# Dummy matmuls in TensorE's early gaps, and later planned times for TensorE's users of transfers, in an attention kernel that feeds an MLP

## The chip, the cores and the metric

The kernel runs on one core of a Trainium2 chip. The core has a matrix engine (TensorE, "PE" in the profile), a vector engine (VectorE, "DVE"), a scalar engine (ScalarE, "ACT"), GpSimd ("POOL") and SyncE ("SP", here only a queue that starts transfers), and 16 DMA engines. Each engine works through its own instruction list in order; semaphores tell one engine that another is done. The metric is the device time of one execution in microseconds (us); lower is better.

## The reference

Eight batches of eight heads, 576 tokens, 64 values per head. Sixteen "beacon" keys and values stand in front of each batch's own. The attention output, 4608 rows of 512 values, goes through a two-layer MLP with a squared relu:

```
k_all = concat([beacon_k, k]);  v_all = concat([beacon_v, v])          # 592 keys
scores = q @ k_all.T / 8;  later keys masked, the beacon keys never
a = exp(scores - max);  a /= a.sum() + 1e-9
x = (a @ v_all), heads side by side                                     # [4608, 512]
h = x @ w_in;  g = relu(h) ** 2;  out = g @ w_out                       # d_ff = 2048
```

Inputs and the output are float32; the kernel computes its matmuls in bfloat16.

## The kernel before

**Tiling.** Keys lie in five tiles (four of 128, one of 80). A pair is two heads; there are 4 pairs per batch and 32 in all. For a pair, TensorE computes the scores with keys on the partitions (L589, op `qk`, into one of two PSUM strips, two matmuls side by side on the two halves of the array), ScalarE takes the exponential into a `pt` tile (L604), VectorE clears the masked part (L614, L618), TensorE multiplies with v (L639, op `av`; v carries a column of ones, which gives the row sums), and VectorE divides (L657, L659, op `norm`). The MLP runs in nine chunks of 512 tokens. A chunk's first layer is 16 steps `s1` (L770, four matmuls of 512 columns each; in chunk 0 two parts), then relu (L786 on ScalarE or L788 on VectorE) and square (L795); its second layer is 4 token tiles of 4 steps `s2` (L805, again four matmuls of 512 columns), an eviction into `osb` and a store (L831, L833, "OUT" below). An `s1` or `s2` step of four 512-column matmuls is called a **quad** below, as is an `s1` step that is cut in two because its tokens wrap around the ring of `xT`.

**Batch 0** is worked in two parts, so that it can start on a part of the tokens: part one is tokens 0 to 239, part two the rest. Its q and k for part one come by the SP and ACT queues (L487), are cast and transposed on TensorE (L451); part two comes by the POOL queue (L419) and is transposed at L454. Batch 1 comes by L419 too. From batch 2 on, q and k come through staging tiles `stg` (eight of them) by the SP queue (L344), are cast on POOL (L299) into `qk_area`, and are transposed by two DMA transposes per batch (L376, ops `trq` and `trk`, each a transfer that the SP queue issues). v comes by L344 too and is cast on POOL into `vb` (L299). From batch 3 on the attention output is transposed into `xT` by five DMA transposes per batch on the SP queue (L690, op `xt`); they wait for the batch's last `norm`. The loads of batch 2 wait until the last quarter of `w_out` has landed.

**What sets the order.** Nothing runs at the listed order of the loops. At build time every piece of work is an `Op` with engines, a duration, a priority and needs, and `Order.run` (lines 67 to 179) plays them through a list of events: whenever an engine is free it takes the released op with the lowest priority number. The sequence that comes out is then written down, one fixed list per engine and queue. Durations in it are the author's figures. A transfer takes `dma` us on one shared DMA time line after a start latency, and counts as seen 1.6 us after that; its users are released at that moment. What the chip then does with the lists is not known to the planner: an engine whose next instruction is not ready waits, and everything behind it waits too.

The names that the change touches: `add_load` (L328, casts of q, k, v), `add_trans` (L372), `add_beacon` (L386), `add_part_loads` (L412), `add_strided` (L429), `add_first_loads` (L477), `add_xt` (L683), and `Order.run`. `g[1]` is the relu buffer of odd chunks, not used before chunk 1; `strips[1]` is the second score strip.

The softmax here doesn't subtract the row's maximum and nothing guards it: scores larger than these inputs give would overflow.

## Time and profile before

| | |
|---|---|
| median of 5 runs | 345.83 us (345.3 to 347.62) |
| profiled execution, its own time | 347.62 us |
| its span, first to last instruction | 345.9 us |
| TensorE busy | 327.6 us, 95% |
| ScalarE / VectorE / GpSimd busy | 194.7 / 169.8 / 90.5 us |
| moved by DMA | 51.88 MB |
| last matmul starts / span ends | 341.5 / 345.9 us |

The profiled execution was the slowest of the five by its own time; its span is 1.7 us shorter than that time. Times in the text are microseconds from the start of the span. A row of the timeline gives start, duration, engine, line, operation, tiles, shape and count, and in brackets how long the engine was idle before it and what ended that. "SPq" and "POOLq" are the queues' own work of issuing transfers. A matmul's end is modelled, so rows overlap by some tenths.

Read off the trace for later use, in us: when the last of the 16 parts of a transfer landed, and when its first user on TensorE started.

| batch | trk issued | trk landed | first scores start | last v cast ends | first `av` starts |
|---|---|---|---|---|---|
| 2 | 67.27 | 73.08 | 73.56 | 82.54 | 81.25 |
| 3 | 93.98 | 100.51 | 101.58 | 108.67 | 108.67 |
| 4 | 122.22 | 127.28 | 129.44 | 135.06 | 136.73 |
| 5 | 155.63 | 160.51 | 163.15 | 174.87 | 173.95 |
| 6 | 188.56 | 196.65 | 197.05 | 208.81 | 207.89 |
| 7 | 223.02 | 227.96 | 229.15 | 242.30 | 241.68 |

The last quarter of `w_out` landed at 50.12. An `av` step needs the last v tile only in its last matmul.

### The profile page before, as it was taken

Reading aid. Unit: us, or ns where it says so; the run is one execution under the profiler, and the core shown is the slowest. Engines: PE = TensorE matmul, PEld = TensorE weight load, DVE = VectorE, ACT = ScalarE, POOL = GpSimd, SP = SyncE. Lnnn points to the kernel's source line nnn. Section 1 sums busy time; section 2 is a strip of 40 time slices with the busy share of each in tenths; the row PEclk is TensorE's granted clock in tenths of the full one; section 3 lists DMA queues with packets and bytes.
Section 4 is the critical chain, followed back from the end, with each engine's and each line's share of the span. In section 5 each row is a group of like instructions: output and inputs, shape, how many; then the busy total and the mean of one; then the engine's idle time right before and its main releaser. Section 6 shows DMA issues by size and latency. Waiting matters only on the chain.

```text
span 345.9 us, 7128 instructions
## 1 busy us (share of the span) xinstructions
PE 327.6 (95%) x2829; PEld 174.1 (50%) x2868; DVE 169.8 (49%) x372; ACT 194.7 (56%) x297; POOL 90.5 (26%) x141
## 2 busy tenths in 40 slices
PE   2799999999999999999999999999999999999995
PEld 1467675544554454444456855544554444444442
DVE  5787984147644974385355546456533302401400
ACT  3795774276646765576566655577536416515611
POOL 9844803305514514150153014312000000000000
PEclk9999999999999999999999999999999999999998
DMA  7999979999999999898799979994015011011002
GB/s 158 210 206 216 206 122 191 211 241 208 189 217 217 213 184 176 198 229 174 152 243 203 178 144 200 217 225 107 2 61 131 0 61 63 0 61 63 0 20 101
DMA packets 145291, 51.88 MB, mean 150 GB/s; under 512 B 132458, under 2 KB 140010, under 8 KB 145258
## 3 DMA queue, kind: packets, MB, share of 16 engines
q1 hardware_dynamic: 135741, 42.45, 59.6%
q0 software_dynamic: 8512, 8.49, 14.7%
q10 hardware_dynamic: 1005, 0.49, 0.5%
q8 instruction: 22, 0.36, 0.4%
q14 instruction: 11, 0.09, 0.1%
HBM read 37.22 MB, written 9.44 MB: 135 GB/s over the span
## 4 chain that ended last, share of the span: by engine, by line
PE 74%; DMA 11%; SPq 4%; ACT 3%; DVE 3%; POOL 2%; issue 1%; POOLq 0%; DVEq 0%; ACTq 0%
PE ps L805 32%; PE ps L770 28%; PE ps L639 8%; DMA stg<-in_v_dram 7%; PE strip L589 6%; SPq L690 3%; ACT pt L604 2%; DMA stg<-in_q_dram 2%; DMA osb<-in_k_dram 1%; DMA out_dram<-osb 1%; POOL vb L299 1%; SPq L344 1%; PE ps L707 1%; DVE g L795 1%; ACT g L786 1%
## 5 line engine op out<-in xcount | busy, mean ns | idle before, releaser
L770 PE MATMUL ps<-xT,w_in 128*128 128x512 bf16 (+3 forms) x690 | 133.2, 340 | 0.8 <-DVE qT L299 0.2
L805 PE MATMUL ps<-w_out,g 128*128 128x512 bf16 x551 | 131.2, 379 | 1.9 <-issue 0.8
L604 ACT ACTIVATE pt<-strip 128x832 bf16<-128x832 f32 (+4 forms) x128 | 103.6, 867 | 39.7 <-PE strip L589 39.7
L786 ACT ACTIVATE g<-ps 128x512 bf16<-128x512 f32 (+2 forms) x128 | 72.0, 562 | 46.6 <-PE ps L770 46.1
L770 PEld LDWEIGHTS <-w_in 128*128 128x128 bf16 x704 | 65.2, 98 | 56.0 <-issue 4.9
L795 DVE TENSOR_TENSOR g<-g 128x1024 bf16<-128x1024 bf16 (+2 forms) x80 | 52.4, 658 | 76.5 <-ACT g L786 75.2
L805 PEld LDWEIGHTS <-g 128*128 128x128 bf16 x576 | 52.4, 98 | 60.8 <-issue 4.0
L299 POOL CAST qk_area<-stg 128x512 bf16<-128x512 f32 (+2 forms) x60 | 39.8, 667 | 56.6 <-DMA stg<-in_k_dram 35.2
L299 POOL CAST vb<-stg 128x512 bf16<-128x512 f32 (+1 forms) x38 | 25.3, 675 | 83.8 <-DMA stg<-in_v_dram 66.3
L297 ACT COPY osb<-ps 128x512 f32<-128x512 f32 x26 | 15.2, 586 | 50.8 <-PE ps L805 44.5
L639 PEld LDWEIGHTS <-pt 128*128 128x128 bf16 (+1 forms) x960 | 36.4, 98 | 14.6 <-issue 3.5
L639 PE MATMUL ps<-vb,pt 128*128 128x65 bf16 (+1 forms) x960 | 40.6, 194 | 1.8 <-POOL vb L299 1.6
L589 PE MATMUL strip<-qT,kT 64*128 64x80 bf16 (+7 forms) x400 | 36.0, 283 | 1.9 <-ACT pt L604 0.6
L659 DVE TENSOR_TENSOR xn<-ps,rcp 128x320 bf16<-128x320 f32 (+2 forms) x64 | 31.5, 492 | 2.5 <-DVE rcp L657 0.2
L614 DVE TENSOR_TENSOR pt<-pt,tri 128x1024 bf16<-128x1024 bf16 (+1 forms) x36 | 24.6, 683 | 13.8 <-ACT pt L604 13.8
L657 DVE RECIPROCAL rcp<-ps 128x5 f32<-128x5 f32 (+2 forms) x64 | 12.2, 191 | 32.1 <-PE ps L639 31.9
L788 DVE TENSOR_SCALAR g<-ps 128x512 bf16<-128x512 f32 (+2 forms) x32 | 19.0, 598 | 10.0 <-PE ps L770 9.3
L589 PEld LDWEIGHTS <-kT 64*128 64x128 bf16 x400 | 12.7, 95 | 21.6 <-issue 16.9
L299 DVE COPY osb<-ps 128x512 f32<-128x512 f32 x10 | 6.9, 692 | 15.4 <-PE ps L805 13.6
L618 DVE TENSOR_TENSOR pt<-pt,tri 80x160 bf16<-80x160 bf16 x32 | 11.5, 359 | 0.0
L344 POOL DMA_DIRECT2D stg<-in_v_dram x10 | 8.6, 863 | 8.5 <-DMA w_in<-in_moe_w_in_dram 6.6
L451 PE MATMUL ps<-ident,qk_area 120*128 120x120 bf16 x16 | 2.3, 300 | 7.6 <-DVE qk_area L299 7.5
(39 smaller groups left out, 69.7 us busy)
## 6 DMA issues: line engine op xcount, KB each, us to landing
out_dram<-osb SPq DMA_DIRECT2D x17, 512.0 KB, 3.4
stg<-in_q_dram SPq DMA_DIRECT2D x24, 256.0 KB, 5.1
stg<-in_k_dram SPq DMA_DIRECT2D x18, 256.0 KB, 5.1
stg<-in_v_dram SPq DMA_DIRECT2D x18, 256.0 KB, 4.5
w_in<-in_moe_w_in_dram POOLq DMA_DIRECT2D x4, 512.0 KB, 11.3
w_out<-in_moe_w_out_dram POOLq DMA_DIRECT2D x4, 512.0 KB, 10.6
stg<-in_v_dram POOLq DMA_DIRECT2D x6, 256.0 KB, 8.4
stg<-in_k_dram SPq DMA_DIRECT2D x6, 224.0 KB, 4.6
```

What stands on the lines that cost most here:

```text
L297: nc.scalar.copy(dst, src)
L299: eng[e].tensor_copy(dst, src)
L589: nc.tensor.matmul(st[:, hj, at:at + t1 - t0], kT[b % 2][hp, pr, 128 * c:128 * c + 128], qT[b % 2][hp, pr, t0:t1], start=True, stop=True,)
L604: nc.scalar.activation(pt[take_pt.held[2]][:, :, off:off + width], st[:, :, 0:width], AF.Exp, bias=0.0, scale=scale)
L614: nc.vector.tensor_tensor(out=d, in0=d, in1=tri[:, m0:m0 + m, :][:, None].to_broadcast([128, 2, m, 128]), op=ALU.min)
L639: nc.tensor.matmul(a[:, at + (t - tl[0]) * (D + 1):at + (t - tl[0] + 1) * (D + 1)], P[0:rr, hj, o:o + 128], vb[b % 2][0:rr, c, 2 * pr + hj ...
L659: nc.vector.tensor_tensor(out=xn[b % 2].rearrange("p t (h d) -> p h t d", d=D)[:, h0:h0 + nh, tl[0]:tl[0] + nt], in0=a[:, :, :, 0:D], in1= ...
L770: nc.tensor.matmul(h[:, lo - spans[0][0]:hi - spans[0][0]], w_in_sb[:, mc, ft * 128:(ft + 1) * 128], xT[:, mc, lo % RING:lo % RING + hi - lo],
L786: nc.scalar.activation(dst, h, AF.Relu, bias=0.0, scale=1.0)
L788: nc.vector.tensor_scalar(out=dst, in0=h, scalar1=0.0, scalar2=None, op0=ALU.max)
L795: nc.vector.tensor_tensor(out=d, in0=d, in1=d, op=ALU.mult)
L805: nc.tensor.matmul(o, G[:, fc, ts * 128:(ts + 1) * 128], w_out_sb[:, fc, :], start=(fc == 0), stop=(fc == NFT - 1))
```

## The change

It has four parts. The planner puts a dummy matmul (`fill`: 256 columns from a zeroed corner of `g[1]`, written to the second half of `strips[1]`) wherever TensorE has nothing to take between 0.3 and 13.0 us of planned time; `g[1]`'s corner is zeroed first by one more memset on VectorE. An op can carry `late`: its users on TensorE are released that much later in the plan than its other users (v casts from batch 1 on 2.0 us, `trq`/`trk` 3.0, `xt` 0.5, batch 1's loads of q and k 1.5). Some planned durations change: `trq`/`trk` 4.5 to 3.7 on the DMA line, first loads, the loads and transposes of batch 0. And the cast of batch 1's beacon keys (L391) waits for pair 3's `norm` of part one. No computation changes; the lists do, on every engine.

```diff
-                 gate=None, dma=0.0, pe_time=0.0, behind=(), sync=()):
+                 gate=None, dma=0.0, pe_time=0.0, behind=(), sync=(), late=0.0):
         self.name = name
+        self.late = late
...
+    FILL_UNTIL = 13.0
...
-                if kind == "done":
+                if kind in ("done", "done_pe"):
                     for u in op.users:
-                        u.left -= 1
-                        if u.left == 0:
-                            release(u)
+                        if ("PE" in u.engs) == (kind == "done_pe"):
+                            u.left -= 1
+                            if u.left == 0:
+                                release(u)
...
                     if best is None:
+                        if e == "PE" and 0.3 < now < self.FILL_UNTIL:
+                            free[e] = now + 0.25
+                            issued.append((Op("fill", "PE", 0.25, self.fill), e, now))
+                            seq += 1
+                            heapq.heappush(events, (free[e], seq, "free", None))
                         continue
...
                     heapq.heappush(events, (seen, seq, "done", op))
+                    seq += 1
+                    heapq.heappush(events, (seen + op.late, seq, "done_pe", op))
...
+    def emit_fill(e):
+        nc.tensor.matmul(strips[1][:, 1, 0:256], g[1][:, 0, 0:128], g[1][:, 0, 0:256], start=True, stop=True)
+
+    order.fill = emit_fill
     add = order.add
 
+    nc.vector.memset(g[1][:, 0, 0:256], 0.0)
     nc.vector.memset(warm, 0.0)
...
         cast[b, x, c] = add(f"cast{b}{x}{c}", engs, {"DVE": 0.6, "POOL": 0.65}, emit_cast,
-                            prio=prio if b else prio - 220.0, deps=deps, give=ld)
+                            prio=prio if b else prio - 220.0, deps=deps, give=ld,
+                            late=2.0 if x == "v" and b > 0 else 0.0)
...
-        trans[b, x] = [add(f"tr{b}{x}", "SP", 4.1, emit, prio=prio, deps=deps, dma=4.5)]
+        trans[b, x] = [add(f"tr{b}{x}", "SP", 4.1, emit, prio=prio, deps=deps, dma=3.7, late=3.0)]
...
         cast[b, "bk"] = bk
+        if b:
+            bk.need.extend(norm_ops[HP - 1, 0])
...
-                        sync=() if pr or n else sync, deps=free, dma=1.07 if b == 0 else 1.5)
+                        sync=() if pr or n else sync, deps=free, dma=0.95 if b == 0 else 1.5, late=1.5 if b else 0.0)
...
-                    tp = add(f"tp{b}.{part}.{pr}{xs}", "PE", 0.1 + (0.1 if b == 0 else 0.075) * ns * len(xs), emit_tp,
+                    tp = add(f"tp{b}.{part}.{pr}{xs}", "PE", 0.1 + (0.06 if b == 0 else 0.075) * ns * len(xs), emit_tp,
...
-                o = add(f"fld{x}{lo}", ("SP", "ACT")[n], (0.45, 0.55)[n], emit, prio=-300.0 + lo, dma=0.68 * (hi - lo))
+                o = add(f"fld{x}{lo}", ("SP", "ACT")[n], (0.45, 0.55)[n], emit, prio=-300.0 + lo, dma={"k": (0.1, 1.7, 0.4), "q": (0.8, 0.5, 1.45)}[x][min(lo, 2)])
...
-            o = add(f"xt{b}.{t}", "SP", 1.32, emit, prio=-50.0 + b, deps=deps, dma=0.64 * n / 128)
+            o = add(f"xt{b}.{t}", "SP", 1.32, emit, prio=-50.0 + b, deps=deps, dma=0.64 * n / 128, late=0.5)
```

In the lists that come out, TensorE has 31 dummies: 14 ahead of the first transposes, then 3, 5, 1, 3 and, right ahead of the first scores of part two, 5. The single one stands between the second pair's scores of part one and their exponential and writes over columns 0 to 255 of that pair's second head in the strip, so those scores are zero there. Counted in the lists, this many quads (chunk 0's half steps counted as one each) stand behind a batch's first scores and behind its first `av`, to the end of the kernel:

| batch | behind first scores, before | after | behind first `av`, before | after |
|---|---|---|---|---|
| 2 | 250 | 249 | 243 | 243 |
| 3 | 229 | 229 | 223 | 224 |
| 4 | 206 | 208 | 200 | 202 |
| 5 | 177 | 183 | 167 | 177 |
| 6 | 148 | 155 | 138 | 149 |
| 7 | 121 | 127 | 109 | 120 |

On the SP queue (b is the beacon's small load, k q v a load of 256 KB or less), from batch 5's loads on:

```
before
b k xt xt xt xt xt q OUT q q q k q k k OUT k trq trk      (xt of batch 3)
b v xt xt xt xt xt v v v v                                (xt of batch 4)
b k q q q q OUT k q k k k trq OUT trk
b v v xt xt xt xt xt v v v                                (xt of batch 5)
b k q q q q k q k OUT k k trq trk
OUT b v v xt xt xt xt xt v v v OUT xt ...                 (xt of batch 6, then 7)
after
b k q q q xt xt xt xt xt q k q OUT k k k trq trk
OUT b v v v v v xt xt xt xt xt b k q q q q k q k k k trq OUT trk
b v v v v OUT v
b k xt xt xt xt xt q q q q k q k k k trq trk
OUT b v v v v v OUT xt xt xt xt xt OUT xt ...
```

Up to batch 4's `trk` both lists hold the same transfers; three stores stand some loads later. On POOL's queue the cast of batch 0's first v tile moves from VectorE to a place between the second and third quarter of `w_in`, and batch 1's q and k loads move behind the casts of batch 0's v.

## The prediction

> **What bounds the kernel now.** I read the page first, then who TensorE waits for, then TensorE, POOL and the SP queue side by side around those waits.

> ```profile
> PE 327.6 (95%) x2829; PEld 174.1 (50%) x2868; DVE 169.8 (49%) x372; ACT 194.7 (56%) x297; POOL 90.5 (26%) x141
> ...
> DMA  7999979999999999898799979994015011011002
> GB/s 158 210 206 216 206 122 191 211 241 208 189 217 217 213 184 176 198 229 174 152 243 203 178 144 200 217 225 107 2 61 131 0 61 63 0 61 63 0 20 101
> ```

> TensorE is busy for 95% of the span, so only its idle time and its place in the work can change. But the transfers are busy as well up to slice 28 (some 240 us). Two bounds run side by side: TensorE's total work, and the time at which each batch's inputs land.

> ```profile
> PE ps L451 <- DVE qk_area L299: 7.5, 3, 3.9
> PE ps L639 <- POOL vb L299: 1.6, 5, 0.4
> ```

> TensorE's waits: 7.5 us at the start, where the first casts wait for the first loads, and later five waits for v casts.

> ```profile
> 13.17 0.49 PE L589 MATMUL strip<-qT,kT 64*128 64x240 bf16 x4
> ...
> 16.57 0.35 PE L589 MATMUL strip<-qT,kT 64*128 64x336 bf16 x4
> ...
> 207.89 0.73 PE L639 MATMUL ps<-vb,pt 128*128 128x65 bf16 x14
> 208.86 0.19 PE L639 MATMUL ps<-vb,pt 80*128 80x65 bf16 x1 [0.25 <-POOL vb L299]
> ```

> The first two rows are scores: 240 + 128 columns per half of the array took 0.49 us at 13 us, and 336 + 80 took 0.35 at 16.6: the array runs slower at first, though the granted clock reads 1.00 from the start. The last two are the wait: the 15th matmul of batch 6's first `av` stands for the last v tile.

> ```profile
> 197.41 0.62 POOL L299 CAST vb<-stg 128x512 bf16<-128x512 f32 x1 [9.48 <-DMA stg<-in_v_dram]
> 198.69 0.61 POOL L299 CAST vb<-stg 128x512 bf16<-128x512 f32 x1 [0.66 <-PE ps L770]
> 206.00 0.62 POOL L299 CAST vb<-stg 128x512 bf16<-128x512 f32 x1 [6.69 <-DMA stg<-in_v_dram]
> ```

> ```profile
> 188.56 4.48 SPq L376 DMA_TRANSPOSE kT<-qk_area  x1
> 193.09 0.57 SPq L343 DMA_DIRECT2D stg<-in_beacon_v_dram  x1
> 193.71 2.17 SPq L344 DMA_DIRECT2D stg<-in_v_dram  x2
> 195.98 5.13 SPq L690 DMA_TRANSPOSE xT<-xn  x4
> ...
> 202.45 2.17 SPq L344 DMA_DIRECT2D stg<-in_v_dram  x3
> ```

> Between v tiles 2 and 3 POOL stands idle for 6.69 us, because SP issues the five `xt` (1.27 us each) in between. SP issues nearly without a gap from 50 to 240 us, so this queue paces the data.

> ```profile
> DMA to landing us min/median/max: 4.9/5.7/8.1
> ```

> This is the `trq`/`trk` line (L376): issue to landing.

> **The change part by part.** The sum is made on the profiled span: last matmul starts at 341.53, span 345.9. The execution's own time of 347.62 is the slowest of five; I subtract the difference from the median, 345.83.

> *Dummies.* 31 matmuls of 256 columns; at the first row's rate (0.49 us for 368 columns) 0.34 us bounds one from above; the warm 240-column L770 matmuls (1.80 us for 16) give 0.11 from below. I take 0.21, nearer to the warm end since consecutive full matmuls overlap: the 14 ahead of the first transposes run from about 1.1 to 4.0, where those transposes start at 3.93, so cost about 0.1. The last five wait for the fourth pair's exponential (14.48 in before) and then delay part two's first scores (14.50) by 0.5 to 1.1 us. Against that, a faster array shortens the packed stretch 12.05 to 16.57: 0.49/368 against 0.35/416 is a ratio of 0.63, at most 1.7 us of 4.5. Together -1.2 to +1.2 at the start, and I take a gain of 0.3. On the end I cost it at nothing: batch 2's loads wait for `w_out` (50.12, a chain of transfers that the dummies do not touch) and its transposes land at 73.08, where TensorE has 0.5 us of slack and loses 1.4 us of earlier waits. If that cover is gone, a start later by over 2 us would show one for one. The extra memset (0.1 us) ends before the first cast's load at 3.55.

> [...]

> *Waits that go.* An undisturbed `av` of 15 takes 0.46 us; start to next start, those of batches 1, 2, 5, 6, 7 took 0.53, 0.91, 0.54, 0.76 and 0.33 more: 3.07 us in all, 1.63 of it behind batch 4.

> *Attention moved ahead.* A quad takes 0.863 us (12 L805 matmuls in 2.59). TensorE ends no earlier than landing + what stands behind that point: the old remainder + added quads - waits that go. For batch 4's scores SP's list is the same in sum, so `trk` lands at 127.28 again: 127.4 + (341.53 - 129.44) + 2 x 0.863 - 1.63 = **339.6**. That is 1.9 us less than 341.53; TensorE's spare 2.16 us in before is what the order gives up.

> For later batches more quads stand behind, so the old landings would hurt: batch 6 gives L + 144.48 + 7 x 0.863 - 1.09 = L + 149.4, and with 196.75 that is 346.2. So the SP queue decides. It gets quicker in the new list:
> - Batch 5: three q loads go out ahead of `xt`, under its 6.4 us of issuing, and one store moves behind `trk`. Three loads at 1.2 us (landings 145.56, 146.77, 147.98) and a store at 1.4, less a start of the rest 1.1 to 1.6 later: 3.4 us. `trk` issues at 152.2, lands 4.9 later, 157.1: 157.2 + 178.38 + 5.18 - 1.63 = 339.1. All v loads follow at once; the last is cast at about 165.0: 165.0 + (341.53 - 174.87) + 10 x 0.863 + 0.41 (one scores step more) - 1.09 = 339.6.
> - Batch 6: the 3.4, a store less among the loads (1.3), no v loads landing ahead of them (1.3): `trk` at 182.6, landing 4.9 to 8.1 later, between 187.5 and 190.7. I take 190.0, near the upper end since this one took 8.1 in before and a store still goes just ahead of it: 339.4. Last v cast near 197.0: 339.3.
> - Batch 7: v loads no longer stand behind `xt` (6.5) and no store lies among its loads (1.5): `trk` lands near 219 instead of 227.96: L + 117.2 = 336.2.

> Bounds of this term: nothing gained (landings as before), 346.2; all gained, 339.6 from batch 4. I take the upper gain, as it is a count of issue rows in one queue. `xt` later costs nothing: batch 5's landed at 203.5 and chunk 5 starts at 221.2. Stores later on SP hold `osb`; they issue 10 us or more before the eviction that reuses it. `norm` waits on `xt` two batches back: covered likewise.

> Sum: -1.94 from 345.83: **343.9 us**. Best case: batch 4's bound a little looser by batch 3's store, -1.5 more: 342.3.

> **The rivals.**
> 1. *Near ties add up, no measurable change.* Five bounds lie between 339.1 and 339.6; each landing is uncertain by 1 to 2 us, the latest counts. One 1 to 3 us late gives 344.9 to 346.9. For it: the spread of 4.9 to 8.1; against: slack in batch 7.
> 2. *Slower: TensorE arrives at batch 6's scores before `kT`.* If `trk` lands after 192.1, the end is later than 341.53. With the old 196.65 it is 346.2, so 350.5 us; at 193.8 it is 347.6, from where the chip would show it. For it: 7 more quads behind; the transposes took 8.1 us there. Against: the SP count above.
> 3. *The dummies' gain reaches the end.* No waits at all: 341.53 less 3.07 and 1.2 of other gaps, less 0.3: 337.0, so 341.3 us. It needs inputs that land 2.6 us earlier from batch 4 on. Against: `w_out` and the same SP list up to there.

> **How the numbers follow.** A measurement here tells a change from none at about 0.5%, 1.7 us. Forecast with its small spread (342.3 to 344.9) 0.45; rival 1 0.25; rival 2 0.22; rival 3 0.08. Of the forecast's 0.45, 0.35 lies under 344.1; with rival 3 faster is 0.43. Same: the forecast's other 0.10 and rival 1's 0.25, less 0.02 of it over 347.56: 0.33. Slower: 0.24, of rival 2 nearly all. Range: 341.9 to 349.0. It reaches half into rival 2 (347.6 to 350.5, so 0.11 left out above) and leaves out half of rival 3 (0.04). The likeliest case's own range is 342.3 to 344.9.

> **What would show it.** Right: no wait of L639 for POOL over 0.3 us from batch 5 on; v casts without a gap of 6 us; `trk` of batch 6 issued near 183, of batch 7 near 214; batch 4's scores start at 127.4 right at the landing. Scores as fast as 0.35 us already at 8 us would show the dummies at work. Wrong: a wait of L589 for DMA of some us at batch 5, 6 or 7 (rival 2), or batch 2's scores later than 75.3.

## The result

| | before | after |
|---|---|---|
| median | 346.29 us (344.6 to 349.64, 47 runs) | 350.12 us (347.98 to 352.16, 26 runs) |
| ratio, 95% interval | | 1.0107 (1.0091 to 1.0123) |
| profiled execution: time / span | 347.62 / 345.9 | 351.72 / 350.0 |
| its last matmul (of `s2`) starts | 341.75 | 345.86 |

The changed kernel is 1.1% slower, 1.1 us above the upper end of the predicted range. (The prediction counted from 345.83, the median of the first five runs of the kernel before, and to 341.53, which is the start of its last matmul but one.) Rival 2 happened: TensorE arrives at scores before their `kT`. Line numbers of the changed kernel are 16 to 19 higher: scores L608 (was L589), `av` L658 (L639), `s1` L789 (L770), `s2` L824 (L805), transposes L393 (L376), `xt` L709 (L690); L283 are the dummies. With them in the kernel, the scores they write over stay zero in the runs below too; no time hangs on that.

The page of the changed kernel:

```profile
PE 333.7 (95%) x2859; PEld 177.6 (51%) x2899; DVE 171.3 (49%) x378; ACT 192.6 (55%) x291; POOL 93.9 (27%) x142
...
DMA  8999969999999999899699969992014011011002
GB/s 168 216 206 217 207 110 219 208 240 205 161 222 224 232 209 159 200 175 226 126 195 210 231 124 200 208 223 49 2 62 123 4 62 60 0 60 62 1 15 105
```

TensorE is busy 6 us longer (dummies, and matmuls at a granted clock of 0.50, shown below). The transfers are as full as before up to slice 28. The chain of causes is in TensorE's waits (total, times, longest):

```profile
PE strip L608 <- DMA kT<-qk_area: 3.9, 2, 2.0
PE ps L658 <- POOL vb L315: 1.9, 3, 1.1
PE strip L283 <- DVE warm L289: 1.1, 1, 1.1
```

The first row is new; before had no wait of scores for a transfer. Of the second, 0.54 us stand behind batch 4, where such waits were to go; 1.1 us of it lie in the first 30 us. Where these waits are, from TensorE's timeline:

```profile
158.74 0.58 PE L608 MATMUL strip<-qT,kT 64*128 64x496 bf16 x4 [2.03 <-DMA kT<-qk_area]
159.26 4.45 PE L789 MATMUL ps<-xT,w_in 128*128 128x512 bf16 x12
...
168.39 0.19 PE L658 MATMUL ps<-vb,pt 80*128 80x65 bf16 x1 [0.54 <-POOL vb L315]
...
195.53 0.58 PE L608 MATMUL strip<-qT,kT 64*128 64x496 bf16 x4 [1.90 <-DMA kT<-qk_area]
```

At batch 5 TensorE stands for 2.03 us, and then twelve `s1` matmuls take 4.45 us that take 2.76 undisturbed. The view by stretches shows why; its columns are the stretch, its length, then busy time and count of PE, PEld, DVE, ACT and POOL, the granted clock, the DMA engines' busy share and GB/s:

```profile
13.10:16.55 3.45, 1.51 (x36) 1.02 (x30) 1.78 (x4) 1.85 (x4) 2.60 (x5) 1.00 1.09 203
16.55:19.96 3.41, 2.66 (x28) 1.60 (x30) 2.90 (x11) 2.62 (x4) 3.08 (x6) 0.50 1.24 205
...
156.50:159.91 3.41, 1.38 (x8) 0.42 (x8) 0.69 (x1) 1.28 (x2) 0.00 (x0) 1.00 1.04 267
159.91:163.32 3.41, 3.41 (x9) 1.17 (x8) 1.39 (x2) 1.75 (x3) 0.84 (x2) 0.50 1.16 229
163.32:166.70 3.38, 3.38 (x22) 1.34 (x20) 2.33 (x4) 2.49 (x4) 1.21 (x3) 1.00 0.93 154
```

A stretch of 3.41 us in which TensorE is busy for 1.38 us (40%) is followed by one at a granted clock of 0.50, called half clock from here on. The same happens at 16.55, behind the 1.51 us of the stretch that follows the last dummies. At batch 6 `trk` goes out behind these rows of the SP queue:

```profile
162.60 8.02 SPq L709 DMA_TRANSPOSE xT<-xn  x5
...
183.93 3.09 SPq L393 DMA_TRANSPOSE qT<-qk_area  x1
187.11 0.53 SPq L852 DMA_DIRECT2D out_dram<-osb  x1
187.74 4.03 SPq L393 DMA_TRANSPOSE kT<-qk_area  x1
```

`trk` is issued at 187.74 (predicted 182.6), 1.8 us after its last cast, and lands at 195.48, 7.74 us later. The five `xt` take 8.02 us to issue; I had counted 6.4.

Times predicted and read off the traces, in us ("issued / landed" for `trk`, then the end of the last v cast):

| | batch 5 | batch 6 | batch 7 | last v cast, batches 5, 6, 7 |
|---|---|---|---|---|
| before | 155.63 / 160.51 | 188.56 / 196.65 | 223.02 / 227.96 | 174.9, 208.8, 242.3 |
| predicted | 152.2 / 157.1 | 182.6 / 190.0 | near 214 / 219 | 165.0, 197, 227 |
| after | 153.83 / 158.70 | 187.74 / 195.48 | 221.84 / 226.74 | 168.3, 202.9, 235.8 |
| after, second profiled execution (e13) | 153.64 / 158.50 | 186.61 / 192.41 | 220.24 / 225.16 | 167.4, 201.7, 235.0 |

Where the 4.1 us from 341.75 to 345.86 come from. TensorE reaches batch 5's scores at 156.71 (158.74 less its wait), 6.4 us earlier than in before. From these scores to the last matmul it takes 182.5 us when nothing waits (e14 below). 156.71 + 182.5 = 339.2, some 2.6 us better than 341.75: that is the gain that the order promised. Then come the wait of 2.03, the slow matmuls (4.45 - 2.76 = 1.7), the v cast 0.5, the wait at batch 6 of 1.9 and some 0.5 more: 345.9. The last of these waits decides: from batch 6's scores e14 takes 150.0 us, and 195.53 + 150.0 = 345.6. Had TensorE lost less ahead of it, it would have waited longer there, as long as that landing stayed where it is.

### The profile page after: what moved, and what is told of

Same layout as the page of the kernel before. It is cut to its first block, busy times and chain, and to the rows that moved or that the text cites. A ratio compares the mean times of both kernels' runs of the same rounds, so it can differ in the third digit from the quotient of the medians.

```text
span 350.0 us, 7186 instructions
## 1 busy us (share of the span) xinstructions
PE 333.7 (95%) x2859; PEld 177.6 (51%) x2899; DVE 171.3 (49%) x378; ACT 192.6 (55%) x291; POOL 93.9 (27%) x142
## 4 chain that ended last, share of the span: by engine, by line
PE 80%; DMA 9%; SPq 5%; POOL 2%; issue 1%; DVE 1%; ACT 1%; POOLq 0%; ACTq 0%
PE ps L824 32%; PE ps L789 31%; PE ps L658 8%; PE strip L608 7%; DMA stg<-in_v_dram 4%; SPq L709 2%; DMA kT<-qk_area 2%; SPq L360 2%; DMA stg<-in_k_dram 2%; DMA stg<-in_q_dram 1%; PE ps L726 1%; PE ps L473 1%; POOL qk_area L438 1%; POOL qk_area L315 0%; ACT g L805 0%
## 5 line engine op out<-in xcount | busy, mean ns | idle before, releaser
L789 PE MATMUL ps<-xT,w_in 128*128 128x512 bf16 (+3 forms) x689 | 135.0, 343 | 0.8
L824 PE MATMUL ps<-w_out,g 128*128 128x512 bf16 x551 | 130.7, 379 | 1.6 <-issue 0.3
L789 PEld LDWEIGHTS <-w_in 128*128 128x128 bf16 x704 | 65.7, 98 | 57.3 <-issue 6.4
L805 ACT ACTIVATE g<-ps 128x512 bf16<-128x512 f32 (+2 forms) x122 | 69.3, 568 | 45.7 <-PE ps L789 43.4
L824 PEld LDWEIGHTS <-g 128*128 128x128 bf16 x576 | 52.8, 98 | 59.6 <-issue 2.0
L315 POOL CAST qk_area<-stg 128x512 bf16<-128x512 f32 (+2 forms) x60 | 40.7, 686 | 64.4 <-DMA stg<-in_k_dram 37.4
L315 POOL CAST vb<-stg 128x512 bf16<-128x512 f32 (+1 forms) x39 | 28.2, 732 | 66.8 <-DMA stg<-in_v_dram 64.5
L658 PEld LDWEIGHTS <-pt 128*128 128x128 bf16 (+1 forms) x960 | 37.1, 99 | 16.7 <-issue 5.9
L658 PE MATMUL ps<-vb,pt 128*128 128x65 bf16 (+1 forms) x960 | 41.1, 195 | 2.7 <-POOL vb L315 1.9
L608 PE MATMUL strip<-qT,kT 64*128 64x80 bf16 (+7 forms) x400 | 35.8, 284 | 4.5 <-DMA kT<-qk_area 3.9
L633 DVE TENSOR_TENSOR pt<-pt,tri 128x1024 bf16<-128x1024 bf16 (+1 forms) x36 | 23.5, 654 | 14.5 <-ACT pt L623 14.5
L807 DVE TENSOR_SCALAR g<-ps 128x512 bf16<-128x512 f32 (+2 forms) x38 | 22.1, 584 | 14.4 <-PE ps L789 13.3
L608 PEld LDWEIGHTS <-kT 64*128 64x128 bf16 x400 | 12.4, 95 | 24.4 <-issue 15.9
L637 DVE TENSOR_TENSOR pt<-pt,tri 80x160 bf16<-80x160 bf16 x32 | 12.8, 399 | 0.0
L283 PE MATMUL strip<-g 128*128 128x256 bf16 x31 | 6.2, 352 | 1.6 <-DVE warm L289 1.1
```

The lines of the kernel that those rows point to most:

```text
L315: eng[e].tensor_copy(dst, src)
L608: nc.tensor.matmul(st[:, hj, at:at + t1 - t0], kT[b % 2][hp, pr, 128 * c:128 * c + 128], qT[b % 2][hp, pr, t0:t1], start=True, stop=True,)
L633: nc.vector.tensor_tensor(out=d, in0=d, in1=tri[:, m0:m0 + m, :][:, None].to_broadcast([128, 2, m, 128]), op=ALU.min)
L658: nc.tensor.matmul(a[:, at + (t - tl[0]) * (D + 1):at + (t - tl[0] + 1) * (D + 1)], P[0:rr, hj, o:o + 128], vb[b % 2][0:rr, c, 2 * pr + hj ...
L789: nc.tensor.matmul(h[:, lo - spans[0][0]:hi - spans[0][0]], w_in_sb[:, mc, ft * 128:(ft + 1) * 128], xT[:, mc, lo % RING:lo % RING + hi - lo],
L805: nc.scalar.activation(dst, h, AF.Relu, bias=0.0, scale=1.0)
```

## The experiments

Each is compared with runs of the kernel before on the same chip; ratios are to those. The question was which part of the change costs the time, and then why the transfers did not come earlier as counted.

**Dummies or order (e1 to e4).** e1 is the changed kernel without dummies:

```diff
-    FILL_UNTIL = 13.0
+    FILL_UNTIL = 0.0
```

> The changed kernel with the dummies left out of the plan (limit 0.0 instead of 13.0); everything else stays. Order theory (the planned length of the two big transposes puts TensorE at batch 6's scores before kT is there): 155 quads still stand behind batch 6's first scores, so the time stays at 349 to 351 us, with two waits of about 2 us for kT. Dummies theory (the dummies spoil the start and the clock): back to 345.5 to 347 us.

Measured: 350.81 us, ratio 1.0118 (1.007 to 1.0166). The loss stays without dummies. Its profiled execution, the fastest of the four at 349.22, does not show the two waits of 2 us that were expected: scores wait 0.2 us for `kT` (batch 5), `av` steps 2.1 us for v casts (batches 5 and 6).

e2 is the kernel before with the dummies and their memset (30 of them come out), and nothing else.

> The kernel before with the dummies and their memset alone. 151 quads stand behind batch 6's first scores instead of 148, which at the old landing of 196.65 allows an end 1.2 us later at most. Order theory: 345.5 to 347.5 us. Dummies theory: 349 to 351 us, with half the granted clock for some us after 16.

Measured: 347.04 us, ratio 1.0007 (0.9993 to 1.0021). Added to this order, the dummies weigh nothing measurable. Of an early clock this run says little: in its profiled execution four scores of 336 columns first take 0.35 us at 21.62, in before at 16.57.

e3 is the changed kernel with one planned length taken back:

```diff
-        trans[b, x] = [add(f"tr{b}{x}", ..., dma=3.7, late=3.0)]
+        trans[b, x] = [add(f"tr{b}{x}", ..., dma=4.5, late=3.0)]
```

> The changed kernel with the planned length of trq and trk back at 4.5 us instead of 3.7; dummies and all the late values stay. 148 quads stand behind batch 6's first scores, as in the kernel before. Order theory: the loss is gone, 344.5 to 346.5 us, no wait of scores for kT over 0.5 us. Dummies theory: 349 to 351 us.

Measured: 346.1 us, ratio 0.999 (0.9962 to 1.0018), no wait for `kT`. The whole loss is gone.

e4 does only that one thing to the kernel before:

```diff
-        trans[b, x] = [add(f"tr{b}{x}", "SP", 4.1, emit, prio=prio, deps=deps, dma=4.5)]
+        trans[b, x] = [add(f"tr{b}{x}", "SP", 4.1, emit, prio=prio, deps=deps, dma=3.7)]
```

> The kernel before with one number changed: the planned length of trq and trk 3.7 us instead of 4.5. No dummies, no late values. 156 quads stand behind batch 6's first scores. Order theory: 349.5 to 352 us, waits for kT of 2 us and more. Dummies theory: 345.5 to 347 us.

Measured: 350.45 us, ratio 1.0109 (1.0077 to 1.014): the whole loss from one number. TensorE's waits in e4:

```profile
PE strip L589 <- DMA kT<-qk_area: 3.1, 2, 2.1
```

and where they are:

```profile
72.57 0.58 PE L589 MATMUL strip<-qT,kT 64*128 64x496 bf16 x4 [1.08 <-DMA kT<-qk_area]
...
100.22 0.58 PE L589 MATMUL strip<-qT,kT 64*128 64x496 bf16 x4 [2.06 <-DMA kT<-qk_area]
```

They stand at batches 2 and 3, not at 5 and 6 as in the changed kernel, nor at batch 6 as the theory has it: the same kind of wait at another place.

So the planned length of `trq`/`trk` does it: each of the two transposes counts 0.8 us less in the plan, and the scores move ahead of what the chip delivers. e3 shows that without this number the loss goes, e4 that it needs nothing else of the change.

**Only the place in TensorE's list (e5, e6).** Both keep the 3.7. e5 takes all `late` values away; e6 raises that of `trq`/`trk` to 8.0, which leaves four quads fewer behind the first scores of batches 5 and 6 than in the changed kernel.

> The changed kernel with all late values at zero; the planned length of trq/trk stays at 3.7 us and the dummies stay. In the lists 185 and 156 quads stand behind the first scores of batches 5 and 6 (changed kernel: 183 and 155), 210 or so behind those of batches 3 and 4 by two more each. Theory (the planned length of the transposes pulls attention forward, the late values push it back a little): 350.5 to 352.5 us, waits for kT of 2 to 4 us at two or more batches. Rival (the late values are what hurts, by moving loads and casts behind one another): back to 346 to 347 us.

Measured: 349.05 us, ratio 1.005 (1.0026 to 1.0074). Neither side's number. In its trace TensorE comes to the scores of batches 2 to 4 right at the landings (0.05 us behind), as the theory has it; but `trk` of batches 5 and 6 lands at 155.76 and 189.06, 3 to 6 us earlier than in the changed kernel. Why is open: its SP list differs by the places of stores and of two or three q loads. It is also faster than the changed kernel (1.0107, and the intervals lie apart): beside the 3.7 the `late` values lost time.

> The changed kernel with the late value of trq/trk at 8.0 us in place of 3.0: only the place of TensorE's scores in its own list moves back, four quads for batches 5 and 6 (179 and 151 quads behind them, changed kernel 183 and 155), the planned transfers stay short. Theory (TensorE comes to the scores before kT has landed): the waits for kT at batches 5 and 6 (2.0 and 1.9 us) go or fall below 0.5 us, no half clock behind batch 5, time 345.5 to 348 us. Rival (the order of the transfers itself makes them land late, whatever stands in TensorE's list): 349.5 to 350.5 us.

Measured: 347.2 us, ratio 1.0021 (0.9994 to 1.0048); no wait for `kT`, TensorE reaches the scores of batches 5 and 6 3.95 and 0.88 us after the landings. As the theory said: TensorE was too early. The transfers of this list landed at 156.99 and 192.53, 1.7 and 2.9 us earlier than in the first profile of the changed kernel, so the place in TensorE's list is not all that differs.

**Is it the half clock, or one store (e9, e10)?** e9 fills the wait with work, meant to keep the clock full:

```diff
             def emit_qk(e, group=group, box=box, i=i):
+                if i == 0 and n == 0 and p in (20, 24):
+                    for _ in range(16 if p == 20 else 24):
+                        nc.tensor.matmul(strips[box["qk"].slots[0]][:, 0, 0:256], ident, w_in_sb[:, 0, 0:256],
+                                         start=True, stop=True)
```

> The changed kernel with dummy matmuls (256 columns, about 0.11 us each) right ahead of the first scores of batch 5 (16 of them) and batch 6 (24), so that the array works through most of the wait for kT. Theory (the landing of batch 6's transposes sets the end; what TensorE loses ahead of it is only a shorter wait there): time as the changed kernel, 349.5 to 351 us, granted clock full from 24 us to the end in the profiled execution, and dummies plus wait at batch 6 come to 3 to 4 us where the wait was 1.9. Rival (the half clock behind batch 5's wait costs its 1.7 us at the end): 348.0 to 348.8 us.

Measured: 350.8 us, ratio 1.0102 (1.0066 to 1.0138); the twelve `s1` matmuls behind batch 5's scores take 2.76 us, so the half clock is gone there. The median is that of the landing theory, but the test is weaker than meant: in the profiled execution, the lowest of its six at 348.77 and inside the rival's range, `trk` of batch 6 was issued at 183.60, the dummies ran out in full (1.91 and 2.78 us), and no wait was left to see. Better evidence lies in the changed kernel's own 27 executions (26 and the profiled one): the eight with a mean granted clock of 0.997 or more have a median of 350.0, the other nineteen 350.4. With half clock goes a difference of 0.4 us there. In e6, where no landing sets the end, the six executions at 0.998 or more have 346.3, the six below 0.996 348.3: there it shows with 1.9 us.

e10 moves one transfer of batch 6: `trq OUT trk` becomes `trq trk OUT`, by moving that one store behind `trk` in the planner's finished list.

> The changed kernel with one transfer moved: the store that SP issues between trq and trk of batch 6 goes out right behind trk. Theory (the landing of batch 6's transposes sets the end, and a store just ahead delays it): trk is issued 1 to 1.4 us earlier and lands 4.9 to 5.9 us after its issue instead of 7.7, about 191 to 193 instead of 195.5; the wait for kT at batch 6 falls below 0.5 us; time 347.5 to 349 us. Rival (the transfers ahead fill the DMA engines, so the place of one store does not matter): 349.7 to 350.5 us.

Measured: 350.44 us, ratio 1.0086 (1.0058 to 1.0114). The local effect came as expected, the time did not. TensorE and SP's queue in the timeline of e10 (lines are 4 higher):

```profile
158.19 0.58 PE L612 MATMUL strip<-qT,kT 64*128 64x496 bf16 x4 [1.81 <-DMA kT<-qk_area]
...
167.13 0.31 PE L662 MATMUL ps<-vb,pt 128*128 128x65 bf16 x5 [1.66 <-POOL vb L319]
...
182.09 3.12 SPq L397 DMA_TRANSPOSE qT<-qk_area  x1
185.30 3.03 SPq L397 DMA_TRANSPOSE kT<-qk_area  x1
```

`trk` landed 4.90 us after its issue, at 190.20, and batch 6's wait was gone. But the inputs of batch 5 had already set the end: 158.19 + 182.5 + 1.9 of waits for its v casts = 342.6; the last matmul started at 343.21. This profiled execution took 349.08; the median of nine is 1.4 us higher, and what is late in those has no trace.

**The changed kernel again (e13).**

> The changed kernel once more, unedited, for a second profiled execution beside the runs that follow. The theory says that in each execution one landing at batches 5 or 6 sets the end, not always the same one: a wait for kT of 1 us or more at one of the two, time 349.5 to 350.8 us. If the profiled execution has no such wait and still ends 3 us late, the theory falls.

Measured: 351.24 us, 0.4 above the expected range; ratio 1.012 (1.0091 to 1.0149).

```profile
158.54 0.58 PE L608 MATMUL strip<-qT,kT 64*128 64x496 bf16 x4 [1.79 <-DMA kT<-qk_area]
166.93 0.31 PE L658 MATMUL ps<-vb,pt 128*128 128x65 bf16 x5 [1.11 <-POOL vb L315]
...
201.78 0.19 PE L658 MATMUL ps<-vb,pt 80*128 80x65 bf16 x1 [1.65 <-POOL vb L315]
```

Batch 5's wait is there again, with the landing at the same place within 0.2 us. Batch 6's wait for `kT` is not; its v casts are late instead. 158.54 + 182.5 + 3.3 (these two and two of 0.25) = 344.3; measured 345.07. Batch 5's wait alone would give 158.54 + 182.5 = 341.0, still ahead of before's 341.75. The wait that decides is the one for batch 6's v: from there e14 takes 142.7 us, and 201.78 + 142.7 = 344.5. So the inputs of batches 5 and 6 are late together, and the one that sets the end changes from one execution to the next: `kT` of batch 6 in the first, v of batch 6 here, v of batch 5 in e10.

**What sets the landings: SP's queue or the DMA engines (e11, e14).** e11 takes the stores off SP's queue (their `dma_start` goes to `nc.gpsimd` with it):

```diff
-                st_ops[u].append(add(f"st{j}.{ts}", "SP", 0.65, emit_st, ...
+                st_ops[u].append(add(f"st{j}.{ts}", "POOL", 1.0, emit_st, ...
```

> The changed kernel with all stores of the output issued by POOL's queue in place of SP's. TensorE's list stays within two quads of the changed kernel's (183, 155 and 127 quads behind the first scores of batches 5, 6 and 7). Theory that the SP queue's issuing (about 1.3 us per store) sets the landings: trk of batches 5 and 6 lands 1.5 to 4 us earlier than 158.7 and 195.5, waits for kT under 0.5 us, time 346 to 348.5 us. Rival (the DMA engines' throughput sets them, since the stores' bytes still have to go): landings within 1 us of the changed kernel's, 349.5 to 351 us. A third case: POOL's casts, queued behind a store that waits for its eviction, come late, and waits for v casts take the place: over 350 us.

Measured: 352.95 us, ratio 1.0178 (1.0133 to 1.0224). The transposes in SP's queue of e11:

```profile
149.46 3.64 SPq L393 DMA_TRANSPOSE qT<-qk_area  x1
153.19 4.93 SPq L393 DMA_TRANSPOSE kT<-qk_area  x1
...
183.77 3.01 SPq L393 DMA_TRANSPOSE qT<-qk_area  x1
186.87 5.22 SPq L393 DMA_TRANSPOSE kT<-qk_area  x1
```

`trk` of batches 5 and 6 was issued 0.6 and 0.9 us earlier than in the changed kernel's first profile, with no store left in this queue, and landed at 159.72 and 196.54, 6.5 and 9.7 us after issue: 1.0 and 1.1 us later. A shorter queue bought nothing. It could not bring the issues much forward either: `trq` went out 0.03 us after its last cast at both batches, and a store in POOL's queue stood ahead of batch 6's last k cast. The time lies above the rival's range, and waits for v casts are 3.1 us (1.9 in the changed kernel), so a part of the third case came with it.

e14 keeps every issue in its place and takes bytes away:

```diff
-  nc.sync.dma_start(out=out[u * 256:u * 256 + 256, :].rearrange("(t p) d -> p t d", p=128), in_=d)
+  nc.sync.dma_start(out=out[u * 256:u * 256 + 256, :].rearrange("(t p) d -> p t d", p=128)[0:16],
+                    in_=d[0:16])
```

> The changed kernel; each of the stores of 256 tokens writes only its first 16 of 128 partitions, so 7/8 of the output but the last chunk's is left out; every issue stays in its place in SP's queue. Some 2.2 stores fall between two batches' transposes, so 1 MB of about 6 MB less in 33.5 us. If the DMA engines' throughput sets the landings (theory now): trk of batches 5 and 6 lands 2 to 5 us earlier than in the changed kernel (158.6 and 192.4 to 195.5), no wait for kT over 0.5 us, time 343 to 347 us. If the issuing of SP's queue sets them: landings within 1 us of the changed kernel's, 349.5 to 351 us.

Measured: 343.71 us, ratio 0.9924 (0.9895 to 0.9953). SP's queue and TensorE in the timeline of e14:

```profile
148.00 3.12 SPq L393 DMA_TRANSPOSE kT<-qk_area  x1
...
155.21 0.58 PE L608 MATMUL strip<-qT,kT 64*128 64x496 bf16 x4
155.72 2.76 PE L789 MATMUL ps<-xT,w_in 128*128 128x512 bf16 x12
...
179.92 3.09 SPq L393 DMA_TRANSPOSE kT<-qk_area  x1
```

One stretch of e14 (DMA share and GB/s are the last two columns):

```profile
122.00:155.00 33.00, 32.67 (x304) 16.23 (x308) 16.72 (x38) 20.61 (x30) 9.88 (x15) 1.00 0.97 181
```

The same stretch of the changed kernel:

```profile
122.00:155.00 33.00, 32.73 (x311) 16.37 (x316) 18.02 (x39) 21.14 (x31) 10.01 (x15) 1.00 0.94 184
```

With the issues unchanged and fewer bytes, `trk` of batches 5 and 6 landed at 152.85 and 184.88, 6 and 8 to 11 us earlier, with no wait for `kT`, while share and GB/s in the stretch are nearly the same: the engines moved as much per us, and less of it was stores. The SP queue's rows for stores did not get shorter: the ten before 240 us take 7.1 us in the changed kernel, 6.9 in e14. That the engines were full is an inference from this; the share alone does not prove it, as it reads up to 1.24 in the rows above. From batch 5's `trk` to batch 6's and batch 7's, the issues are 32.9 and 34.5 us apart in before, 33.9 and 34.1 after, 33.7 and 34.5 in e11, and 31.9 and 31.0 in e14. Over the two together e14 takes 62.9 us, and every profiled execution that stores the whole output 64.6 (e19) to 68.8 (e3): the order of the list changes this pace too, but none comes down to e14's. Its last matmul started at 337.66, 182.5 us after batch 5's scores: the remainder without waits that is used above.

The kernel before already showed that this queue is not always what `trk` waits for. Rows of POOL and of SP's queue:

```profile
154.98 0.63 POOL L299 CAST qk_area<-stg 80x512 bf16<-80x512 f32 x1 [2.30 <-DMA stg<-in_k_dram]
...
155.63 3.16 SPq L376 DMA_TRANSPOSE kT<-qk_area  x1
```

SP had been idle for 0.56 us when batch 5's `trk` went out at 155.63, 0.03 us after the last k cast ended, and that cast had waited for its load. It is the same in the changed kernel: cast to 153.80, `trk` at 153.83.

**What is worth keeping (e12, e7, e15 to e19).** e12 is e6 without dummies, e7 is e3 without dummies (`FILL_UNTIL = 0.0` in both).

> The changed kernel with late 8.0 for trq/trk (attention a few quads later) and without dummies. Without dummies the array comes to full clock later, once, and is not throttled again by the sparse stretch behind the dummies. If the dummies' early clock is worth something where no landing covers it: 0.5 to 1.5 us slower than with them (347.2). If they only move the half clock: within 0.5 us of 347.2. If they harm: 345.5 to 346.5 us, a tie with the kernel before or just under it.

Measured: 347.2 us, ratio 0.9999 (0.9971 to 1.0026); e6 had 1.0021. Within the intervals the dummies do nothing here.

> The changed kernel with the planned length of trq/trk back at 4.5 us and without dummies; late values and the rest stay. 203, 175, 146 and 118 quads stand behind the first scores of batches 4 to 7, fewer than before (206, 177, 148, 121). No wait for kT; waits for v casts of 2 to 3 us as before. Theory: 345 to 346.5 us, no different from the kernel before (the dummies weigh under 0.5 us). If the dummies help at this order, whose inputs have 2 to 3 us of slack: 346.5 to 347.5 us.

Measured: 345.21 us, ratio 0.9941 (0.9918 to 0.9965): faster than before, and than e3 with dummies. To be sure of that, e15 (e3 again) and e16 (e7 again) ran on one chip, with e17, which is e16 with all `late` values at zero.

> The changed kernel with the planned length of trq/trk back at 4.5 us, dummies in, once more, to stand beside the next run on one chip. If the dummies cost time at this order: ratio to the kernel before 0.997 to 1.001, 0.3% or more above the next run. If the two earlier ratios differed by the chip or by chance: within 0.2% of it.

> The same without dummies, once more. If the order with late values and the old planned length is what makes it faster: ratio to the kernel before 0.992 to 0.997 again. If that was chance: 0.998 to 1.001.

> The run above with all late values at zero: 207, 178, 150 and 121 quads stand behind the first scores of batches 4 to 7 (203, 175, 146 and 118 with them; kernel before 206, 177, 148 and 121). If the late values earn the gain, by leaving TensorE 2 to 4 us of other work at each batch: 0.997 to 1.002 of the kernel before, waits for v casts back. If the gain comes from the other planned lengths and the start: 0.992 to 0.997 as with them.

Measured: e15 346.3 us, 1.0002 (0.9978 to 1.0026); e16 344.8 us, 0.9948 (0.9926 to 0.997); e17 347.78 us, 1.0034 (1.0015 to 1.0053). Two findings. In this order, in which TensorE mostly comes 1.7 us or more after the landings, the kernel with dummies takes 1.5 us more. TensorE in e15:

```profile
7.62 0.34 PE L608 MATMUL strip<-qT,kT 64*128 64x240 bf16 x4 [0.27 <-DVE qT L315]
...
19.36 0.53 PE L608 MATMUL strip<-qT,kT 64*128 64x336 bf16 x4
```

and in e16:

```profile
7.65 0.49 PE L608 MATMUL strip<-qT,kT 64*128 64x240 bf16 x4 [0.89 <-ACT qT L313]
...
19.28 0.35 PE L608 MATMUL strip<-qT,kT 64*128 64x336 bf16 x4
```

With dummies four scores of 240 columns take 0.34 us at 7.62 (0.49 without), where TensorE mostly waits for casts anyway; from 16.88 to 20.29, where it is busy throughout (3.41 us), the granted clock is 0.50 and four scores of 336 columns take 0.53 us (0.35 without, at a granted clock of 1.00). The last pair's scores of batch 0 start at 23.11 with them, at 21.01 without. The three of e15's twelve executions with a mean granted clock of 0.998 or more have a median of 344.6, no more than e16; the other nine 347.0. So the half clock goes with the loss, though the lists differ a little as well (148 and 146 quads behind batch 6's first scores), and e15's profiled execution, one of its slowest, has a wait of 1.28 us for `kT` at batch 5. And the `late` values gain 0.9% at this planned length. e18 puts them alone on the kernel before; e19 is e16 with 4.5 and 3.5 in place of 3.0 and 2.0.

> The kernel before with nothing but the late values (v casts 2.0, trq/trk 3.0, xt 0.5, batch 1's loads 1.5): no dummies, all planned lengths as before. From batch 4 on the same number of quads stands behind the first scores (203, 175, 146, 118) as in e16. If the late values alone earn the gain: 0.992 to 0.997 of the kernel before, waits for v casts at 1 us or less in all. If the other planned lengths are needed for it: 0.998 to 1.003.

> e16 with late 4.5 for trq/trk and 3.5 for v casts in place of 3.0 and 2.0 (203, 174, 145 and 117 quads behind the first scores of batches 4 to 7). e16 has 1 us of waits for v casts left and lands 0.3 to 2.5 us ahead of its scores, so at most about 1 us is to be had: 0.990 to 0.997 of the kernel before. If TensorE's end of the kernel now lacks work to put beside the last attention: 0.997 to 1.002.

Measured: e18 344.97 us, 0.9945 (0.9917 to 0.9973); e19 344.59 us, 0.9927 (0.9904 to 0.995). Both beat before; e19 has the lowest ratio of all that compute the whole output, though it and e18 and e16 lie within each other's intervals. In e18 2.0 us of waits for v casts are left, where 1 us or less was expected; e19 has none in its list. Where the `late` values take effect, by stretches of before:

```profile
20.00:40.00 20.00, 19.01 (x318) 14.00 (x316) 16.72 (x42) 14.79 (x28) 10.57 (x15) 1.00 1.21 210
...
74.00:130.00 56.00, 54.61 (x512) 27.64 (x520) 36.87 (x75) 36.60 (x53) 21.17 (x30) 1.00 1.05 212
130.00:240.00 110.00, 108.24 (x971) 58.27 (x985) 58.37 (x119) 68.45 (x97) 30.59 (x48) 1.00 0.97 191
```

and of e18:

```profile
20.00:40.00 20.00, 19.98 (x333) 15.45 (x330) 16.17 (x40) 16.33 (x32) 10.99 (x15) 1.00 1.21 213
...
74.00:130.00 56.00, 55.92 (x537) 28.03 (x534) 35.57 (x75) 35.68 (x51) 21.40 (x31) 1.00 1.11 204
130.00:240.00 110.00, 109.33 (x973) 57.76 (x972) 57.13 (x116) 69.62 (x99) 31.79 (x47) 1.00 1.04 190
```

TensorE's idle time falls from 0.99 to 0.02, from 1.39 to 0.08 and from 1.76 to 0.67 us: other work stands where it had waited.

## Why the prediction was wrong

- **"SP issues nearly without a gap ..., so this queue paces the data": the step that failed.** From it came landings of 157.1 and 190.0 and last v casts at 165.0, 197 and 227. They came 1.5, 2.4 to 5.5, and 2.4 to 8.8 us later than that. I had counted issue rows in one queue as time saved (3.4 us, then more), a store at 1.4 us; ten store rows take 7.1 us in the changed kernel. e11 shortens the queue and gains nothing; e14 leaves it as it is, moves fewer bytes, and `trk` lands at 152.85 and 184.88, 6 us and more earlier. So fewer bytes brought the inputs forward and fewer rows did not, though the place of one store just ahead of `trk` counts at its own batch (190.20 instead of 195.48 in e10). In e11 the rows of `trk` grew (4.93 and 5.22 us, 2.98 and 4.03 in the changed kernel), so a row's length is no fixed price; what makes it long was not tested. The kernel before already had SP idle ahead of batch 5's `trk` (rows behind e14 above). Nor did issuing the stores from POOL's queue make the transfers of SP's land sooner: e11's `trk` landed 6.5 and 9.7 us after issue, the changed kernel's 4.9 and 7.7.
- **The near tie, taken as a safe one.** I put five bounds between 339.1 and 339.6 and let rival 1 have "one 1 to 3 us late". The landings were late together, which is rival 2. Its formula held: L + 149.4 with the landing of 195.48 gives 344.9 for the last matmul but one, which started at 345.64. Its place was right in the first profiled execution. In both, `kT` of batch 5 is late too (158.7 and 158.5); in the second, v of batch 6 sets the end in place of `kT`.
- **The remainder.** 178.38 + 6 quads - 1.63 = 181.9 predicted, 182.2 when counted to the last matmul; 182.5 in e14. Quads of 0.863 us, and the waits that go, were right as a count of work.
- **"Waits that go", 1.63 behind batch 4.** They go only if the casts come early enough. With TensorE 10 quads ahead at the `av` steps, they came back: 0.5 us behind batch 5's scores in the first profiled execution, 3.3 in the second.
- **The half clock was not in the sum.** Behind the wait at batch 5 it slows the matmuls by 1.7 us (twelve in 4.45 against 2.76, granted clock 0.50), in one of the two profiled executions. I had not priced it. There batch 6's landing set the end all the same, and between executions with and without it the difference is 0.4.
- **The dummies, "on the end I cost it at nothing".** Right, in this order: 350.8 without and 350.1 with them (e1), 1.0007 when added to before (e2). The gain of 0.3 that I took for the start was wrong in kind: the packed stretch "12.05 to 16.57" got no faster clock to its end, but half clock from 16.55 to 23.38 (four scores of 336 columns in 0.53 us at 19.08, 0.35 at 19.04 in before). Where the cover is gone, the kernel with them takes 1.5 us more (e15 against e16), a little over my upper end of 1.2. The lower end of my range, 341.9, counts on some 3.9 us gained by the dummies; no run shows such a gain, only these differences, and 347.2 both with and without them in e6 and e12.
- **Batch 4.** Predicted at 127.4 right at the landing; measured 126.38, with the landing at 125.74, 1.5 earlier than counted. This bound was looser than I took it, as in my best case, and did not decide.
- **What was to show it.** The v casts stand together now, as said, and the scores take 0.34 us already at 7.4 us; but `trk` of batches 6 and 7 was issued 4 to 8 us later than "near 183" and "near 214", and the waits named as the sign of rival 2 are there.

Left open: why e5's transfers come earlier than the changed kernel's, and what is late in those executions of e1, e9 and e10 that take 350 us and more, since their profiled ones, at 349, show no wait for `kT` at batch 6 over 0.3 us.

## What to carry to other kernels

A plan made at build time holds only as well as its durations: the transposes took 4.9 to 8.1 us from issue to landing in the kernel before (up to 9.7 in e11), and a planned length cut from 4.5 to 3.7 made an in-order TensorE stand before the inputs of a later batch, for the whole 1.1%. Distance in the plan between a landing and its first user on the bound engine (`late` values here) gained 0.55% by itself (e18) and 0.9% beside the other changes (e16 against e17), more than the early dummies did; beside the short planned length it gained nothing (e5). Before counting issue rows of a queue as time saved, look at whether the queue is idle ahead of the transfer in question and what it waits for there. At a busy share of 0.94 to 1.05, fewer bytes brought the landings forward (e14) and fewer issues in the queue did not (e11).

## What the runs showed of the hardware

```profile
156.11:159.52 3.41, 1.62 (x10) 0.45 (x9) 0.69 (x1) 1.50 (x3) 0.00 (x0) 1.00 1.09 276
159.52:162.93 3.41, 3.41 (x23) 1.51 (x22) 1.83 (x3) 3.01 (x5) 0.62 (x1) 1.00 1.09 216
```
